# LSH attention with spatial gating: score tiles released by the minimum, two buffers of split rows, four of exponentials

## The chip, the cores and the metric

The kernel runs on one core of a Trainium2 chip. The metric is the device time of one execution in microseconds (us). A core has five engines with a program of their own each, run in order: TensorE (PE; its weight loads are listed as PEld), VectorE (DVE), ScalarE (ACT), GpSimd (POOL), and SyncE (SP), which here only issues transfers. TensorE writes to PSUM, a small memory of banks; everything else lies in SBUF. The kernel before took 742.45 us (median of 3 runs, 740.67 to 743.2).

## What is computed

Attention with 4 batches of 8 heads, 768 rows of 64 numbers. Each query and key gets a hash of 6 bits (signs of a projection), and a query sees only keys of its own hash. The outcome of all heads goes through a gated MLP with a product along the rows.

```python
q_bucket = np.sum((q @ proj > 0) * 2 ** np.arange(6), axis=-1)     # k_bucket alike
scores = np.where(q_bucket[..., :, None] == k_bucket[..., None, :], scale * q @ k.T, -1e9)
attn = np.exp(scores - np.max(scores, axis=-1, keepdims=True))
attn = attn / (np.sum(attn, axis=-1, keepdims=True) + 1e-09)
x = attn @ v                                                       # (4, 768, 512)
h = np.maximum(x @ w_in, 0.0)
u, v = h[..., :512], h[..., 512:]
v_n = (v - mean(v)) / np.sqrt(var(v) + 1e-06)
v_s = np.einsum('ts,bsd->btd', w_spatial, v_n) + b_spatial[None, :, None]
out = (u * v_s) @ w_out
```

## The kernel before

**Order.** The program is not written in the order in which it runs. Every step is registered with `op(engine, duration, function, predecessors, on=buffers, rank=...)`. `timetable` (line 117) then places all of them with the stated durations, each engine taking the ready operation of the lowest rank, and at the end the functions are called in the order of the planned starts. So each engine's order is fixed when the program is built; on the chip an engine runs its list in order and waits by semaphores for data and for buffers. A buffer is an object `buf(name, n)`: its `new()` waits for the users of the one `n` places before.

**Tiles.** Two heads make a pair, so there are 16 pairs (`p`), four to a batch. A pair has 6 steps (`i`), one for each 128 rows. `scores` (line 448) runs 16 products for a step, four passes over two halves of 384 columns for two heads: three with q and k split into fp16 parts (tile `hl`, from `split_qk`), one with hash rows (tile `hk`, from `hash_rows`), whose product puts other buckets far down. The outcome is one PSUM tile `sp` for each head, two banks each, and there are two of them, so that a step needs both tiles of the step before to be free.

**A step by queries** (`by_queries`, line 461): VectorE takes the minimum of the scores scaled by a negative factor (line 473, its elementwise output goes as bf16 into the `ex` tile and is not used); ScalarE takes the exponential of the scores, reading PSUM, into `ex` (line 476); ScalarE rounds it to fp16 in `pp` (line 480); VectorE or GpSimd writes the rest beside it (line 484); SP issues a transposing transfer `pt<-pp` (line 488); and some steps later `weighted` multiplies `pt` with the split `v` on TensorE (line 594). Heads 2, 4 and 6 (pairs 1 to 3) go by keys instead (`by_keys`), with a maximum found ahead (`row_max`) and an exponential straight from the scores (line 509).

**Buffers.** `ex` and `pp` have 3 each (`EB`, `PB`), `pt` 8 (`PTB`), `hl` 3, `hk` 3 tiles taken in turn. `load_qk` (line 302) brings q and k of a pair, one buffer.

**Ahead of a pair.** At step 1 of pair p `hash_rows(p + 2)` is registered, at step 2 `split_qk(p + 2)`, at step 3 `load_qk(p + 3)`. Hash rows go through TensorE and VectorE and are put into `hk` by 8 small transfers that GpSimd issues (line 356). After the last `weighted` of a pair comes `normalize`, in step 3 of the next pair.

**The MLP.** When a batch's four pairs are done, its products (`mlp_units`, all through line 689) are registered with a high rank number, so that the planner puts them where TensorE would be free. The last batch's products over its first three pairs are made beforehand (`partial_units`) and kept in tiles of `hl` and `qk`. The weights are brought and split by `weights()` from 30 us of the plan on.

Of the kernel before, what the change touches and what calls it, by code (L numbers as in the profile page):

```python
# [18 lines left out]
P = 128  # L19
D = 64  # L20
# [15 lines left out]
def lsh_attention_spatial_gating(  # L36
# [194 lines left out]
    ws = [const.tile([P, NT, S], F16, name=f"ws{i}") for i in range(2)]  # L231
# [4 lines left out]
    def weights():  # L236
# [5 lines left out]
        raws = buf("u", UB).new()  # L242
        vi, vo, vs = (x.rearrange("(c p) f -> p c f", p=P) for x in (w_in, w_out, w_sp))
# [7 lines left out]
        for i, (src, dst, m, f, key) in enumerate(jobs):  # L251
# [41 lines left out]

            t = op("A", 0.3 * z, high, t, on=hold, rank=R_W)
# [30 lines left out]
    def hash_rows(p, *after):  # L325
        qk, k = held["qk", p], buf("hk", NHK).new()
# [24 lines left out]
        for j in range(4):  # L351
            for e in range(2):
                q, eng = HQ_FIRST[e] if p == 0 else HQ_REST

                def move(j=j, e=e, eng=eng):
                    eng.dma_start(  # L356
                        out=hk[p % NHK][D * e:D * e + 2 * NB, 1 - j // 2, (j % 2) * HS:(j % 2 + 1) * HS],
                        in_=sg[1][32 * j + 16 * e:32 * j + 16 * e + 2 * NB, :])
                at["hk", p].append(op(q, 0.53 if q == "G" else 0.75, move, t, on=[g1, k], rank=3, land=2.8 if q == "G" else 1.8))

    def split_qk(p, *after):
        qk, h = held["qk", p], buf("hl", 3).new()
        held["hl", p] = h

        def high():
            st["hl", p] = wk.tile([P, 4, S], F16, tag="hl", bufs=3, name=f"hl{p}")
            nc.scalar.activation(st["hl", p][:, 1:3], st["qk", p], AF.Copy, scale=SQ)

        t = op("A", 1.42, high, at["qk", p], *after, on=[qk, h], rank=4)
        at["hl", p] = [t] + [  # L370
            op("V", 0.9, lambda to=to, part=part, frm=frm: nc.vector.scalar_tensor_tensor(
                out=st["hl", p][:, to], in0=st["qk", p][:, part], scalar=SQ, in1=st["hl", p][:, frm],
                op0=ALU.mult, op1=ALU.subtract), t, on=[qk, h], rank=4)
            for to, part, frm in ((0, 1, 2), (3, 0, 1))]
# [60 lines left out]
    def sums(ps, p, rows, passes, queries, halves=(0, 1), heads=(0, 1)):  # L435

        for a, (x, y, last) in enumerate(passes):
            for c in halves:
                cs = slice(c * HS, (c + 1) * HS)
                for e in heads:  # L440
                    byq_ = queries or 2 * p + e not in KEYS
                    r = slice(D * e, D * e + D - (last and byq_))
                    src = hk[p % NHK] if last else st["hl", p]
# [17 lines left out]
    def by_queries(p, i, e, g, t, sc):  # L461
# [6 lines left out]
        def low():  # L468
            if i == 0:
                st["nb", n] = wk.tile([P, NT], F32, tag="nb", bufs=6, name=f"nb{n}")  # L470
            ex = st["e32", n, i] = wk.tile([P, 2, HS], F32, tag="ex", bufs=EB, name=f"ex{n}_{i}")
            jk = ex.rearrange("p c k -> p (c k)").bitcast(BF16)[:, :S].rearrange("p (c k) -> p c k", c=2)
            nc.vector.tensor_scalar(jk, st["sc", p, i][e], -ISQ, None, op0=ALU.mult, op1=ALU.min, accum_out=st["nb", n][:, i:i + 1])  # L473

        def exp():
            nc.scalar.activation(st["e32", n, i], st["sc", p, i][e], AF.Exp, bias=st["nb", n][:, i:i + 1], scale=ISQ)  # L476
# [15 lines left out]
        t = op("A", 0.83, exp, t, on=[sc, hx], rank=(g, 0.1 + 0.1 * e))  # L492
# [52 lines left out]
    def max_row(p):  # L545
        for e in keys(p):
# [20 lines left out]
            def move(n=n, e=e):  # L567
                nc.sync.dma_start(out=hk[p % NHK][D * e + D - 1:D * e + D, 1, :], in_=st.pop(("mt", n)))

# [132 lines left out]
    def partial_units():  # L702
# [4 lines left out]
        hv_ = [buf("hl", 3).new() for _ in range(2)]  # L707
        hu = buf("qk", 1).new()
        held["vpart"], held["upart"] = hv_, hu
        on = [held["xt", b * NPAIR + c] for c in pairs]  # L710
        after = [at["xt", NP - 2]]

        for i in range(NT):
            def copy(c, i=i):
                if i % 3 == 0:
                    st["vb", i // 3] = wk.tile([P, 4, S], F16, tag="hl", bufs=3, name=f"vpart{i}").rearrange("p a s -> p (a s)").bitcast(F32)
# [5 lines left out]
        for d in range(NF):  # L722
            def copy(c, d=d):
                if d == 0:
                    st["ub"] = wk.tile([P, NF, HS], F32, tag="qk", name="upart")
                nc.scalar.copy(st["ub"][:, d], c[0])

            def then(t, c, pool, d=d, copy=copy):
                at["upart", d] = op("A", 0.4, lambda: copy(c), t, on=[hu], rank=1, gives=pool)
            group(f"upp{d}", HS, u_products(b, d, 0, pairs), then, on, after, bank_m, rank=8.9)  # L730

    def mlp_units(b):
# [102 lines left out]
        def u_unit(d, h):  # L835
# [9 lines left out]
            def then(t, c, pool):  # L845
                def plus():
                    make()
                    nc.vector.tensor_tensor(out=u[h][:, d], in0=c[0], in1=st["ub"][:, d], op=ALU.add)  # L848
# [6 lines left out]
                if part:  # L855
                    t = op("V", 0.45, plus, t, at["upart", d], on=[hu[h], held["upart"]], rank=1, gives=pool)
# [4 lines left out]
        def s_unit(d, h):  # L861
# [3 lines left out]
            if d == 0:  # L865
                hg[h] = (buf("hl", 3) if last and h else buf("g", 1)).new()
            hy = buf("sy", 2).new()

            def then(t, c, pool):
# [6 lines left out]
                def high():  # L876
                    if d == 0 and last and h == 1:
                        g1 = wk.tile([P, 4, S], F16, tag="hl", bufs=3, name="g_1").rearrange("p a s -> p (a s)")
# [41 lines left out]
    EB, PB, PTB, XTB, VB, UB = 3, 3, 8, 6, 6, 2  # L920
# [7 lines left out]
    R_W = 0.9  # L928
    W_FROM, W_EVERY = 30.0, 3.6
# [11 lines left out]
    weights()  # L941
# [6 lines left out]
    for g in range(STEPS + LAG):  # L948
# [15 lines left out]
        if p < NP:  # L964
# [79 lines left out]
```

## Time and profile before

| | before |
|---|---|
| median of 3 runs | 742.45 us |
| profiled execution, time | 743.31 us |
| profiled execution, span | 741.5 us |
| TensorE busy | 638.3 us |
| VectorE busy | 557.7 us |
| ScalarE busy | 459.4 us |
| GpSimd busy | 411.4 us |
| mean TensorE clock granted | 0.935 |

A row of a group of instructions reads: line, engine, operation, output<-inputs, sizes, count | busy us, mean ns of one | idle time of the engine just before them and who ended it. A row of waits reads: who waited <- for whom: us in total, times, longest. Names with a q (SPq) are an engine's queue. In a stage's row each engine has its busy us and its number of instructions, and then come the granted clock, the share of the DMA engines' time, and GB/s. A row of the timeline has start, duration, and in brackets the idle time before it.

### The profile page before, as it was taken

How to read it: one execution, taken by the hardware profiler on the slowest of the kernel's cores; microseconds unless marked ns; L12 is line 12 of the kernel's file. 1: busy time of each engine (PE TensorE's matmuls, PEld its weight loads, DVE VectorE, ACT ScalarE, POOL GpSimd, SP SyncE). 2: the span in 40 equal slices, each digit the busy share in tenths (PEclk: the TensorE clock that was granted, in tenths of full speed). 3: DMA queues.
4: the chain of work that ended last, by engine and by line, in shares of the span. 5: the costliest groups of instructions: out<-in, count | busy, mean ns of one | idle time of the engine just before them, and what ended most of it. 6: DMA issues, size and time to landing. Idle time of an engine off the chain costs nothing. (4 is left out here: it accounts for less than half of the span.)

```text
span 741.5 us, 16949 instructions
## 1 busy us (share of the span) xinstructions
PE 638.3 (86%) x6667; PEld 376.2 (51%) x6667; DVE 557.7 (75%) x1014; ACT 459.4 (62%) x707; POOL 411.4 (55%) x446
## 2 busy tenths in 40 slices
PE   3778799886988878698998799989889899989997
PEld 1445557563545455454554456545445555545553
DVE  6788987769999988877887989797968785382250
ACT  3767656777886865576676777676756775432212
POOL 5346665778657685856683858583745551233100
PEclk9889957887999998889999999999999999999999
DMA  5799784799998889799999789989698879001102
GB/s 179 148 167 203 165 177 100 159 226 177 188 202 145 150 179 188 160 181 204 172 181 184 155 174 175 185 177 204 128 173 172 135 128 163 3 1 44 44 1 85
DMA packets 318260, 110.85 MB, mean 149 GB/s; under 512 B 305124, under 2 KB 308196, under 8 KB 318180
## 3 DMA queue, kind: packets, MB, share of 16 engines
q1 hardware_dynamic: 314244, 108.62, 74.6%
q0 software_dynamic: 3840, 1.12, 0.8%
q8 instruction: 52, 0.85, 0.5%
q14 instruction: 28, 0.23, 0.1%
q10 hardware_dynamic: 96, 0.04, 0.0%
HBM read 27.94 MB, written 6.29 MB: 46 GB/s over the span
## 5 line engine op out<-in xcount | busy, mean ns | idle before, releaser
L476 ACT ACTIVATE ex<-sp,nb 128x768 f32<-128x768 f32 x174 | 155.0, 899 | 113.2 <-DVE ex L473 111.0
L484 POOL TENSOR_TENSOR pp<-ex,pp 128x768 f16<-128x768 f32 x66 | 116.8, 1770 | 109.7 <-ACT pp L480 107.3
L473 DVE TENSOR_SCALAR_CACHE_REDUCE ex<-sp 128x768 bf16<-128x768 f32 x174 | 160.0, 949 | 22.0 <-PE sp L445 20.2
L594 PE MATMUL pv<-vp,pt 128*128 128x65 f16 (+1 forms) x3132 | 125.3, 197 | 48.6 <-DMA pt<-pp 35.3
L484 DVE TENSOR_TENSOR pp<-ex,pp 128x768 f16<-128x768 f32 x108 | 126.2, 1174 | 53.3 <-ACT pp L480 53.0
L445 PE MATMUL sp<-hl 64*128 64x384 f16 x1152 | 137.7, 355 | 28.7 <-ACT ex L476 25.6
L594 PEld LDWEIGHTS <-pt 128*128 128x128 f16 x3132 | 111.7, 100 | 94.8 <-DMA pt<-pp 51.1
L480 ACT CAST pp<-ex 128x768 f16<-128x768 f32 x174 | 141.4, 828 | 22.6 <-DMA pt<-pp 22.2
L445 PEld LDWEIGHTS <-hl 64*128 64x128 f16 x1188 | 64.3, 100 | 93.5 <-issue 65.1
L689 PE MATMUL sps<-ws,vn 128*128 128x384 f16 x576 | 102.6, 330 | 0.7 <-DVE sy L874 0.5
L356 POOL DMA_DIRECT2D hk<-sg x120 | 64.1, 540 | 22.4 <-PE ups L689 7.4
L689 PEld LDWEIGHTS <-vn 128*128 128x128 f16 x576 | 54.8, 99 | 37.5 <-issue 4.8
L689 PE MATMUL ops<-wo,g 128*128 128x512 f16 x288 | 66.7, 381 | 1.9 <-DVE u L848 1.9
L886 POOL TENSOR_TENSOR sy<-sy,u 128x384 f32<-128x384 f32 x24 | 28.2, 1175 | 63.6 <-DVE sy L874 63.2
L445 PE MATMUL sp<-hk 63*128 63x384 f16 (+1 forms) x384 | 61.0, 355 | 2.8 <-DMA hk<-sg 2.8
L689 PE MATMUL ups<-xt,wi 128*128 128x384 f16 x348 | 61.5, 327 | 1.6 <-DVE sy L874 1.2
L689 PE MATMUL vps<-wi,xt 128*128 128x512 f16 x234 | 56.6, 380 | 1.9 <-DVE sg L341 1.1
L874 DVE SCALAR_TENSOR_TENSOR sy<-sps,bt 128x384 f32<-128x384 f32 x32 | 17.7, 552 | 43.9 <-PE sps L689 41.2
L689 PEld LDWEIGHTS <-wi 128*128 128x128 f16 x384 | 36.3, 98 | 26.0 <-issue 3.5
L882 ACT CAST g<-sy 128x384 f16<-128x384 f32 x32 | 16.4, 512 | 44.6 <-POOL sy L886 24.2
L689 PEld LDWEIGHTS <-g 128*128 128x128 f16 x288 | 26.9, 98 | 32.1 <-issue 3.1
L445 PEld LDWEIGHTS <-hk 63*128 63x128 f16 (+1 forms) x420 | 29.8, 104 | 24.0 <-issue 11.6
(103 smaller groups left out, 857.2 us busy)
## 6 DMA issues: line engine op xcount, KB each, us to landing
qk<-kq SPq DMA_DIRECT2D x16, 768.0 KB, 6.3
out<-o SPq DMA_DIRECT2D x24, 256.0 KB, 2.0
v<-v SPq DMA_DIRECT2D x13, 384.0 KB, 4.0
pt<-pp SPq DMA_TRANSPOSE x174, 4.6
raw<-w_in SPq DMA_DIRECT2D x8, 256.0 KB, 3.6
raws<-w_in SPq DMA_DIRECT2D x8, 256.0 KB
hk<-sg POOLq DMA_DIRECT2D x120, 9.0 KB, 3.3
vf<-v SPq DMA_DIRECT2D x3, 384.0 KB
```

What stands on the lines that cost most here:

```text
L356: eng.dma_start(out=hk[p % NHK][D * e:D * e + 2 * NB, 1 - j // 2, (j % 2) * HS:(j % 2 + 1) * HS], in_=sg[1][32 * j + 16 * e:32 * j + 16 * ...
L445: nc.tensor.matmul(ps[e][:, c - halves[0]], lhsT=src[r, l, rows], rhs=src[r, m, cs], start=(a == 0), stop=(a == len(passes) - 1))
L473: nc.vector.tensor_scalar(jk, st["sc", p, i][e], -ISQ, None, op0=ALU.mult, op1=ALU.min, accum_out=st["nb", n][:, i:i + 1])
L476: nc.scalar.activation(st["e32", n, i], st["sc", p, i][e], AF.Exp, bias=st["nb", n][:, i:i + 1], scale=ISQ)
L480: nc.scalar.copy(st["pp", n, i][:, 0], st["e32", n, i])
L484: eng.tensor_tensor(out=st["pp", n, i][:, 1], in0=st.pop(("e32", n, i)), in1=st["pp", n, i][:, 0], op=ALU.subtract)
L594: nc.tensor.matmul(o, lhsT=l, rhs=m, start=(i == 0 and k == 0), stop=(i == NT - 1 and k == len(todo_) - 1))
L689: nc.tensor.matmul(c[0], lhsT=l(), rhs=r(), start=(j == 0), stop=(j == len(products) - 1))
L874: nc.vector.scalar_tensor_tensor(out=y[0], in0=c[0], scalar=1.0 / (SN * SW), in1=bt[:, hs], op0=ALU.mult, op1=ALU.add)
L882: nc.scalar.copy(gt[h][0][:, d], y[0])
L886: t1 = op(*POST[last], lambda: either(t1).tensor_mul(y[0], y[0], u[h][:, d]), t, done["u", d, h], on=[hy, hu[h]], rank=2)
```

## The change

Four things are changed together. The minimum's instruction writes the scaled scores as fp32 into `ex`, and the exponential reads them there with a scale of -1; it no longer reads PSUM, so the next step's scores wait for the minimum alone. `ex` and `pp` get 4 buffers, `pt` 9. `hl` and `hk` get 2 buffers, with pair 1's rows in the tiles of the weights `ws`, which are written later; hashing and splitting of pair p + 1 is registered at step 0 of pair p (from pair 3 on), the load of pair p + 2 at step 1, and `weights()` after step 11. The last batch's partial sums are kept in other tiles (`hl`, `qk`, `v32`, `hk`).

```diff
-    NHK = 3
-    hk = [const.tile([P, 2, S], F16, name=f"hk{i}") for i in range(NHK)]
-    for i, t in enumerate(hk):
+    ws = [const.tile([P, NT, S], F16, name=f"ws{i}") for i in range(2)]
+    flat = [t.rearrange("p c s -> p (c s)") for t in ws]
+    hk = [const.tile([P, 2, S], F16, name=f"hk{i}") for i in range(2)]
+    hkt = lambda p: hk1 if p == 1 else hk[(p + 1) % 2 if p else 0]
+    hk1 = flat[1][:, :2 * S].rearrange("p (g s) -> p g s", g=2)
+    for i, t in enumerate(hk + [hk1]):
...
+        place = [buf("hl1", 1).new(), buf("hk1", 1).new()]
...
+            if key == "ws":
+                hold = hold + place
...
     def split_qk(p, *after):
-        qk, h = held["qk", p], buf("hl", 3).new()
+        qk, h = held["qk", p], (buf("hl", 2) if p != 1 else buf("hl1", 1)).new()
...
+            if p == 1:
+                st["hl", p] = flat[0][:, :4 * S].rearrange("p (g s) -> p g s", g=4)
+            else:
+                st["hl", p] = wk.tile([P, 4, S], F16, tag="hl", bufs=2, name=f"hl{p}")
...
-            jk = ex.rearrange("p c k -> p (c k)").bitcast(BF16)[:, :S].rearrange("p (c k) -> p c k", c=2)
-            nc.vector.tensor_scalar(jk, st["sc", p, i][e], -ISQ, None, op0=ALU.mult, op1=ALU.min, accum_out=st["nb", n][:, i:i + 1])
+            nc.vector.tensor_scalar(ex, st["sc", p, i][e], -ISQ, None, op0=ALU.mult, op1=ALU.min, accum_out=st["nb", n][:, i:i + 1])
 
         def exp():
-            nc.scalar.activation(st["e32", n, i], st["sc", p, i][e], AF.Exp, bias=st["nb", n][:, i:i + 1], scale=ISQ)
+            nc.scalar.activation(st["e32", n, i], st["e32", n, i], AF.Exp, bias=st["nb", n][:, i:i + 1], scale=-1.0)
...
-        t = op("A", 0.83, exp, t, on=[sc, hx], rank=(g, 0.1 + 0.1 * e))
+        t = op("A", 0.83, exp, t, on=[hx], rank=(g, 0.1 + 0.1 * e))
...
-        hv_ = [buf("hl", 3).new() for _ in range(2)]
-        hu = buf("qk", 1).new()
+        hv_ = [buf("hl", 2).new(), buf("qk", 1).new()]
+        hu = [buf("v32", 1).new(), buf("hk", 2).new()]
...
-    EB, PB, PTB, XTB, VB, UB = 3, 3, 8, 6, 6, 2
+    EB, PB, PTB, XTB, VB, UB = 4, 4, 9, 6, 6, 2
...
+    AHEAD = 1
...
-    weights()
...
-            if i == 1 and p + 2 < NP:
+            if i == AHEAD and p + 2 < NP and p < 2:
                 hash_rows(p + 2, now)
-            if i == 2 and p + 2 < NP:
                 split_qk(p + 2, now)
-            if i == 3 and p + 3 < NP:
+            if i == AHEAD + 1 and p + 3 < NP and p < 2:
                 load_qk(p + 3, now)
+            if i == 0 and 2 < p + 1 < NP and p > 2:
+                hash_rows(p + 1, now)
+                split_qk(p + 1, now)
+            if i == 1 and 4 < p + 2 < NP:
+                load_qk(p + 2, now)
+            if g == 2 * NT - 1:
+                weights()
```

More of the change, by code (lines that the diff above doesn't have):

```diff
@@ L356, in move @@
                     eng.dma_start(
[L357 removed]
+                        out=hkt(p)[D * e:D * e + 2 * NB, 1 - j // 2, (j % 2) * HS:(j % 2 + 1) * HS],
                         in_=sg[1][32 * j + 16 * e:32 * j + 16 * e + 2 * NB, :])
@@ L442, in sums @@
                     r = slice(D * e, D * e + D - (last and byq_))
-                    src = hk[p % NHK] if last else st["hl", p]
+                    src = hkt(p) if last else st["hl", p]
                     l, m = (x, y) if byq_ else (y, x)
@@ L715, in copy @@
                 if i % 3 == 0:
-                    st["vb", i // 3] = wk.tile([P, 4, S], F16, tag="hl", bufs=3, name=f"vpart{i}").rearrange("p a s -> p (a s)").bitcast(F32)
+                    t = (wk.tile([P, 4, S], F16, tag="hl", bufs=2, name=f"vpart{i}").rearrange("p a s -> p (a s)").bitcast(F32) if i == 0 else
+                         wk.tile([P, 2, S], F32, tag="qk", name=f"vpart{i}").rearrange("p a s -> p (a s)"))
+                    st["vb", i // 3] = t
                 nc.scalar.copy(st["vb", i // 3][:, (i % 3) * F2:(i % 3 + 1) * F2], c[0])
@@ L724, in copy @@
                 if d == 0:
-                    st["ub"] = wk.tile([P, NF, HS], F32, tag="qk", name="upart")
-                nc.scalar.copy(st["ub"][:, d], c[0])
+                    ub[0] = wk.tile([P, 2 * NT, D], F32, tag="v32", name="upart").rearrange("p a d -> p (a d)")
+                nc.scalar.copy(st["ub"](d), c[0])
             def then(t, c, pool, d=d, copy=copy):
-                at["upart", d] = op("A", 0.4, lambda: copy(c), t, on=[hu], rank=1, gives=pool)
+                at["upart", d] = op("A", 0.4, lambda: copy(c), t, on=[hu[d // 2]], rank=1, gives=pool)
             group(f"upp{d}", HS, u_products(b, d, 0, pairs), then, on, after, bank_m, rank=8.9)
@@ L847, in plus @@
                     make()
-                    nc.vector.tensor_tensor(out=u[h][:, d], in0=c[0], in1=st["ub"][:, d], op=ALU.add)
+                    nc.vector.tensor_tensor(out=u[h][:, d], in0=c[0], in1=st["ub"](d), op=ALU.add)
                 def relu():
@@ L855, in then @@
                 if part:
-                    t = op("V", 0.45, plus, t, at["upart", d], on=[hu[h], held["upart"]], rank=1, gives=pool)
+                    t = op("V", 0.45, plus, t, at["upart", d], on=[hu[h], held["upart"][d // 2]], rank=1, gives=pool)
                 done["u", d, h] = op("A", 0.4, relu, t, done.get(("u", 0, h)), on=[hu[h]], rank=1, gives=None if part else pool)
@@ L865, in s_unit @@
             if d == 0:
-                hg[h] = (buf("hl", 3) if last and h else buf("g", 1)).new()
+                hg[h] = (buf("hl", 2) if last and h else buf("g", 1)).new()
             hy = buf("sy", 2).new()
@@ L877, in high @@
                     if d == 0 and last and h == 1:
-                        g1 = wk.tile([P, 4, S], F16, tag="hl", bufs=3, name="g_1").rearrange("p a s -> p (a s)")
+                        g1 = wk.tile([P, 4, S], F16, tag="hl", bufs=2, name="g_1").rearrange("p a s -> p (a s)")
                         gt[h] = [g1[:, k * NF * HS:(k + 1) * NF * HS].rearrange("p (d q) -> p d q", d=NF) for k in range(2)]
```

8 lines of the change are left out of this document (4 added, 4 removed).

## The prediction

> **What bounds the kernel now.** I read the page's head, the stages, TensorE's waits, one step in the timeline, and then who is late on the engines that feed it. The page's span and engine sums, and the stages by window (length, busy time and count of each engine, granted TensorE clock, DMA share, GB/s):
>
> ```profile
> span 741.5 us, 16949 instructions
> PE 638.3 (86%) x6667; PEld 376.2 (51%) x6667; DVE 557.7 (75%) x1014; ACT 459.4 (62%) x707; POOL 411.4 (55%) x446
> ...
> 0.00:12.00 12.00, 3.94 (x20) 1.06 (x22) 8.13 (x12) 3.78 (x4) 6.46 (x17) 1.00 0.48 170
> 12.00:52.00 40.00, 26.65 (x315) 15.84 (x313) 30.69 (x61) 25.00 (x34) 15.65 (x19) 0.85 0.84 167
> 52.00:160.00 108.00, 93.30 (x908) 65.06 (x902) 86.77 (x181) 70.69 (x125) 73.29 (x90) 0.82 0.81 164
> 160.00:473.00 313.00, 268.65 (x3145) 156.21 (x3144) 266.20 (x463) 221.40 (x331) 213.59 (x220) 0.94 0.93 178
> 473.00:625.00 152.00, 136.68 (x1639) 78.88 (x1639) 121.14 (x215) 103.88 (x151) 82.40 (x81) 0.99 0.88 162
> 625.00:742.00 117.00, 109.11 (x655) 59.12 (x651) 44.78 (x86) 34.63 (x67) 19.97 (x20) 0.99 0.11 36
> ```
>
> The rows cut the run into start-up, pair 0, pairs 1 to 3 (by keys), 4 to 11, 12 to 15, and a tail. The tail is TensorE alone: 109 of 117 us busy, DMA at 0.11. What it runs are products of the MLP that the attention found no room for. So any gap of TensorE closed during the attention shortens the tail or the attention by as much: the end is TensorE's work, 638.3, plus its gaps, 741.5 - 638.3 = 103.2 us. No other engine is full: from 12 to 625 VectorE is busy 504.8 of 613 us, ScalarE 421.0. The question is which gaps close. TensorE's waits (total, times, longest):
>
> ```profile
> PE pv L594 <- DMA pt<-pp: 35.3, 32, 4.5
> PE sp L445 <- ACT ex L476: 25.6, 30, 4.2
> PE pv L594 <- DVE x L623: 12.9, 8, 2.9
> PE hp L334 <- DMA qk<-kq: 5.8, 1, 5.8
> ...
> PE sp L445 <- ACT ex L509: 2.8, 2, 2.1
> ```
>
> The second row is the wait that the first part of the change is aimed at: the next scores wait for the exponential (L476) that still reads the old ones. One such step in the timeline (start, duration):
>
> ```profile
> 184.46 0.94 DVE L473 TENSOR_SCALAR_CACHE_REDUCE ex<-sp 128x768 bf16<-128x768 f32 x1
> ...
> 185.33 0.94 DVE L473 TENSOR_SCALAR_CACHE_REDUCE ex<-sp 128x768 bf16<-128x768 f32 x1
> 185.44 1.78 ACT L476 ACTIVATE ex<-sp,nb 128x768 f32<-128x768 f32 x2 [2.91 <-DVE ex L473]
> ...
> 186.39 0.32 PE L445 MATMUL sp<-hl 64*128 64x384 f16 x1 [2.33 <-ACT ex L476]
> ...
> 187.27 2.07 PE L445 MATMUL sp<-hl 64*128 64x384 f16 x11 [0.56 <-ACT ex L476]
> ```
>
> The first minimum ends at 185.40 and TensorE gets that tile at 186.39; the second ends at 186.27, its tile is taken at 187.27. Released by the minimum, with the same 0.05 us of hand-over (185.40 to 185.44), a tile is free about 0.94 us sooner.
>
> **The change part by part.** The groups it touches (count, busy, mean ns, idle before and its releaser):
>
> ```profile
> L476 ACT ACTIVATE ex<-sp,nb 128x768 f32<-128x768 f32 x174 | 155.0, 899 | 113.2 <-DVE ex L473 111.0
> L473 DVE TENSOR_SCALAR_CACHE_REDUCE ex<-sp 128x768 bf16<-128x768 f32 x174 | 160.0, 949 | 22.0 <-PE sp L445 20.2
> L484 DVE TENSOR_TENSOR pp<-ex,pp 128x768 f16<-128x768 f32 x108 | 126.2, 1174 | 53.3 <-ACT pp L480 53.0
> L480 ACT CAST pp<-ex 128x768 f16<-128x768 f32 x174 | 141.4, 828 | 22.6 <-DMA pt<-pp 22.2
> ...
> L371 DVE SCALAR_TENSOR_TENSOR hl<-qk,hl 128x768 f16<-128x768 f32 x32 | 34.7, 1107 | 0.8 <-ACT hl L367 0.8
> L367 ACT ACTIVATE hl<-qk 128x1536 f16<-128x1536 f32 x16 | 23.7, 1479 | 4.2 <-DMA qk<-kq 3.7 <-issue 0.5
> L623 DVE TENSOR_TENSOR x<-pv,rv 128x384 f32<-128x384 f32 x32 | 16.8, 547 | 0.1
> L509 ACT ACTIVATE ex<-sp 128x768 f32<-128x768 f32 x18 | 14.5, 803 | 17.8 <-PE sp L445 17.7
> ```
>
> (1) Score tiles are released by the minimum. Thirty waits of 25.6 us lose up to 0.94 us each. In the timeline eight of them are longer (the longest keeps 4.2 - 0.94 = 3.3, the quoted 2.33 keeps 1.4); together they keep 7.3 us. Gain 25.6 - 7.3 = **18.3 us**; bounds 0 (all of it turns up as a wait elsewhere) and 25.6. The 2.8 behind L509 stays, as heads by keys keep their exponential on the scores. What is late next is VectorE's minimum itself, which in program order stands behind its other work.
>
> (2) The exponential reads SBUF. Nearest rows: a 128x768 pass of ScalarE took 803 ns from PSUM (L509, without a bias tile) and 828 from SBUF (L480), so 25 ns more, 174 times: 4.4 us of ScalarE, which idles 113 us in front of these very instructions. I take 0 on the path, bounds 0 and 4.4, the latter if that idle time were gone. [...]
>
> (3) The minimum writes 768 f32 in place of 768 bf16. No row shows this instruction with f32. L623 reads PSUM and writes f32: 547 ns for 384 elements; L473 takes 949 for 768. The 384 more cost 402 ns, about 1.05 ns an element whichever type is written. I take no change; bounds 0 and the 225 ns by which L484, f32 operands of the same size on VectorE, exceeds it (1174), which is 39 us over 174.
>
> (4) A fourth `pp` and `ex` and a ninth `pt`. The cast (L480) waits 22.2 us, 22 times, about 1.0 us each, for a transpose to have read the `pp` of three tiles before. With four it waits for the transpose one place earlier: 128x1536 f16 are 393 KB, 2.2 us at the 178 GB/s of the middle stage (an estimate), more than the mean wait, so nearly all of it goes. The way to TensorE:
>
> ```profile
> SPq L488 <- DVE pp L484: 118.8, 58, 8.4
> ...
> SPq L308 <- DVE hl L371: 8.0, 3, 4.9
> ```
>
> SP's queue, which issues the transposes, waits 118.8 us for the rest (L484); this waits 53.0 for the cast (its row above); the cast 22.2 for buffers. Of VectorE's 53.0, 22.2 at most is of this origin, 42%; of TensorE's 35.3 behind transposes that is 14.8. I take half of the 22.2, **11 us**; bounds 0 and 22.2.
>
> (5) Split rows and hash rows in two buffers. Nothing is added: as many hash products, splits and DMA issues. From pair 4 on they move from steps 1, 2 and 3 of the pair two before to steps 0 and 1 of the pair just before. The chain to be ready in time:
>
> ```profile
> qk<-kq SPq DMA_DIRECT2D x16, 768.0 KB, 6.3
> ...
> hk<-sg POOLq DMA_DIRECT2D x120, 9.0 KB, 3.3
> ...
> L356 POOL DMA_DIRECT2D hk<-sg x120 | 64.1, 540 | 22.4 <-PE ups L689 7.4
> ```
>
> Eight issues on GpSimd are 4.3 us, the landing 3.3, the split 1.5 + 2 x 1.1 = 3.7; one after the other 11.3 us. The lead was eleven steps and is six; a step of pairs 4 to 15 takes (625 - 160) / 72 = 6.5 us, so 39 us remain. The buffer that is written was last read by the step just before, already past on TensorE, so the eight issues hold nothing on GpSimd's queue that they do not hold now. The `qk` load goes by SP's queue: it waits there for the split (L371), with transposes behind it: 8.0 us in 3 of 16 loads today. The distance between split and load stays one step, so I take 0; bounds 0 and 16 us, if each of the 11 loads from pair 5 on waited the longest 4.9 (54 us) and TensorE felt 35.3 / 118.8 of it. On the other side, today hash, split, load, the `v` split and the normalisation crowd steps 1 to 3; spread out they could gain some us, which I don't count.
>
> (6) Pair 1's rows lie in `ws`, and the weights come after them in the list. The last scores of pair 1 in the timeline, and the first writes of `ws` (min/median/max, first and last start):
>
> ```profile
> 80.00 0.48 PE L445 MATMUL sp<-hk 64*128 64x384 f16 x2
> ...
> L292 ACT ACTIVATE ws<-raw x6: 507/520/525, 122.4 to 162.4; 128x384 f16<-128x384 f32 x6
> ```
>
> They end at 80.5 us and the writes begin at 122.4: no wait. The partial sums of the last batch go to other tiles whose readers are done by then; 0.
>
> **Sum.** The profiled execution took 743.3 us (741.5 of span and 1.8 around it); 743.3 - 18.3 - 11 = **714 us**. The median of the runs shown, 742.45, is 0.9 below that execution; the range covers it.
>
> **The rivals.**
>
> *The clock comes back as well.* TensorE was granted 0.85, 0.82 and 0.94 in three stages and 0.99 after. At 1.00 their matmuls lose 0.15 x 26.65 + 0.18 x 93.3 + 0.06 x 268.65 = 37 us. If shorter gaps restore half, the time is 714 - 18 = 696. For it: 0.99 where TensorE is 90% busy (136.68 of 152), 0.94 where it is 86%. Against it: it was granted 0.62 in a stretch without any gap:
>
> ```profile
> 100.00:125.00 25.00, 25.00 (x181) 16.87 (x181) 18.67 (x42) 12.65 (x21) 12.64 (x13) 0.62 0.64 140
> ```
>
> [...] Chance 0.13.
>
> *The transposes take the wait over.* DMA is at 0.93 from 160 to 473. If scores come sooner but transposes land no sooner, term 4 gives nothing and a fifth of term 1 returns as waits of L594: 743.3 - 18.3 x 0.8 = 729. For it: the largest wait is already theirs. Against it: SP's queue waits for data 118.8 us. Chance 0.16.
>
> *The change doesn't shorten anything.* The planner's pace (`T_QUERIES` and the rest) is unchanged, so as many MLP products stand between two steps in TensorE's order; only 25.6 of 103.2 us of gaps name the exponential. If both terms just move to other rows: 741 to 745. Chance 0.09.
>
> *Slower: the f32 write shares a path with GpSimd.* The place is L473, on the loop scores, minimum, scores. L484 on VectorE averages 1174 ns, GpSimd working beside it; were L473 to go to the same, 174 x 0.225 = 39 us come onto the loop: 714 + 39 = 753. It decides from 29.3 / 174 = 0.17 us on, a mean of 1.12 us. Against it: L623's f32 writes (547) show no such excess. Chance 0.10.
>
> **How the numbers follow.** Forecast 0.52, clock 0.13, transposes 0.16, nothing 0.09, slower 0.10. About 0.3% is what a measurement of this kernel can tell from no change. Faster 0.52 + 0.13 + 0.16 = 0.81, same 0.09, slower 0.10. The forecast's own bounds are 743.3 - 25.6 - 22.2 = 695 and 714 + 16 + 4 = 734. The range goes from 692, into the clock's case, to 742, into the nothing's; left out are the slower case and the edges of two, under 0.2.
>
> **What would show it.** `PE sp <- ACT ex L476` is gone, and a wait for `DVE ex` of at most 8 us stands there. L480's wait for transposes falls under 6 us, L594's from 35 to about 24. L476 takes 920 to 945 ns, L473 still 949. TensorE's busy time stays at 638 within 6. L473 above 1.12 us, a `qk` load that waits for L371 for more than 2 us in most pairs, or L594's wait grown beyond 45 us would each prove me wrong.

## The result and the profile after

The changed kernel took 748.18 us (median of 20 runs, 741.99 to 757.74), the kernel before 741.35 on the same chip (median of 20); the ratio is 1.013, with a 95% interval of 1.0095 to 1.0165. It is slower by 1.3%, where 714 us were forecast. The medians here and below are of all runs, while the ratios leave out the slow executions of a kernel, so a ratio need not be the quotient of the two medians beside it. The profiled execution took 750.24 us. Head of the page after, then its stages, cut as those of before were:

```profile
span 748.4 us, 16873 instructions
...
PE 631.0 (84%) x6667; PEld 370.7 (50%) x6667; DVE 558.5 (75%) x1009; ACT 463.5 (62%) x707; POOL 419.0 (56%) x451
```

```profile
12.00:52.00 40.00, 28.38 (x311) 16.41 (x308) 34.81 (x65) 25.38 (x34) 25.54 (x30) 0.81 0.85 176
52.00:160.00 108.00, 91.52 (x989) 64.31 (x988) 94.06 (x189) 76.77 (x127) 63.05 (x77) 0.90 0.81 166
160.00:473.00 313.00, 258.40 (x3115) 150.75 (x3112) 260.93 (x455) 220.24 (x331) 208.25 (x211) 0.95 0.93 177
473.00:625.00 152.00, 132.91 (x1566) 75.09 (x1563) 116.64 (x207) 100.86 (x145) 95.89 (x96) 0.97 0.85 157
625.00:749.00 124.00, 115.94 (x688) 63.03 (x684) 43.98 (x85) 36.44 (x70) 19.86 (x20) 1.00 0.12 36
```

TensorE works 7.3 us less than before (631.0 for 638.3; the granted clock's mean is 0.945 for 0.935), and its gaps grew from 103.2 to 748.4 - 631.0 = 117.4 us. Length less TensorE's time, stage by stage: from 160 to 473 us 44.4 before and 54.6 after, from 473 to 625 us 15.3 and 19.1. The windows are the same in time, not in work. Cut at the work instead, from the first scores of pair 4 to the last scores of all, the rows are these, before and after:

```profile
160.30:619.40 459.10, 399.89 (x4721) 232.27 (x4722) 383.60 (x670) 321.61 (x476) 294.94 (x299) 0.95 0.91 172
```

```profile
146.90:618.50 471.60, 393.82 (x4711) 227.78 (x4712) 384.51 (x673) 328.85 (x486) 312.39 (x318) 0.95 0.92 173
```

TensorE's gaps there are 59.2 us before and 77.8 after. So the loss lies in pairs 4 to 15, which go by queries and which the change was made for. TensorE's largest waits after (total, times, longest), then those of SP's queue for a transpose's data and for the split:

```profile
PE pv L601 <- DMA pt<-pp: 49.5, 41, 2.5
PE sp L453 <- DVE ex L480: 16.1, 19, 1.8
PE pv L601 <- DVE x L630: 15.6, 9, 5.2
...
SPq L495 <- DVE pp L491: 79.2, 46, 5.2
...
SPq L313 <- DVE hl L379: 11.2, 4, 4.1
```

The wait for the exponential is gone, as forecast, and what stands in its place is the minimum, 16.1 us for 25.6. But the products with transposes, which waited 35.3 us, wait 49.5, although SP's queue now waits 79.2 us for VectorE's rest in place of 118.8. The groups that were touched:

```profile
L483 ACT ACTIVATE ex<-ex,nb 128x768 f32<-128x768 f32 x174 | 158.0, 934 | 120.8 <-DVE ex L480 120.5
L480 DVE TENSOR_SCALAR_CACHE_REDUCE ex<-sp 128x768 f32<-128x768 f32 x174 | 160.0, 949 | 24.9 <-PE sp L453 24.8
L491 DVE TENSOR_TENSOR pp<-ex,pp 128x768 f16<-128x768 f32 x103 | 126.4, 1231 | 57.7 <-ACT pp L487 56.7
L487 ACT CAST pp<-ex 128x768 f16<-128x768 f32 x174 | 138.4, 822 | 0.6
```

The cast's 22.2 us of waits for buffers have become 0.6 us of idle time, but the next link, VectorE's wait for the cast, is no shorter (53.0 before, 56.7 now), and ScalarE waits 120.5 us for the minimum where it waited 111.0. The waits moved along the chain.

**Where the attention stood.** The first scores of pair 4 in the trace before (matmuls: min/median/max in ns, first and last start), and after:

```profile
L445 PE MATMUL sp<-hl x12: 497/524/524, 160.3 to 161.8; 64*128 64x384 f16 x12
```

```profile
L453 PE MATMUL sp<-hl x12: 319/322/333, 146.9 to 148.2; 64*128 64x384 f16 x12
```

There the change's execution was 13.4 us ahead, and in a phase of a higher clock (322 ns for 524 in the median; granted were 1.00 from 146.9 to 148.3 us, and 0.50 from 160 to 162 before). Not all of this lead need be the change's. Three kernels below (e9, e10, e11) run the program of before up to pair 4, and their executions reach it at 156.6, 152.1 and 152.6 us. They were granted clocks of 0.88, 0.94 and 0.89 over the first 152 us, where the execution of before had 0.84 over its first 160. So 3.7 to 8.2 us of the 13.4 can be the execution alone. The last scores of all in the timeline before, and after:

```profile
619.37 1.15 PE L445 MATMUL sp<-hl 64*128 64x384 f16 x12
```

```profile
618.48 1.15 PE L453 MATMUL sp<-hl 64*128 64x384 f16 x12
```

The lead is down to 0.9 us. What is left to do then is products of the MLP. The windows of their line alone (length, TensorE busy and count, weight loads, clock, DMA, GB/s), before and after:

```profile
0.00:619.00 619.00, 192.37 (x941) 86.13 (x942) 0.92 0.88 171
619.00:742.00 123.00, 109.86 (x597) 57.71 (x595) 0.99 0.17 43
```

```profile
0.00:618.00 618.00, 185.03 (x892) 82.52 (x893) 0.93 0.88 171
618.00:749.00 131.00, 117.68 (x645) 62.56 (x643) 1.00 0.15 40
```

The attention took as long as before with some 48 products fewer among its steps, and these lie behind it. From the last scores to the end are 122.1 us for 594 products before and 129.9 for 642 after, 0.206 and 0.202 us for each. How many products stand ahead of the last scores is settled by TensorE's order, which the planner fixes when the program is built.

### The profile page after: what moved, and what is told of

It reads as the page before. It is cut to its first block, busy times and chain, and to the rows that moved or that the text cites. A ratio compares the mean times of both kernels' runs of the same rounds, so it can differ in the third digit from the quotient of the medians.

```text
span 748.4 us, 16873 instructions
## 1 busy us (share of the span) xinstructions
PE 631.0 (84%) x6667; PEld 370.7 (50%) x6667; DVE 558.5 (75%) x1009; ACT 463.5 (62%) x707; POOL 419.0 (56%) x451
## 4 chain that ended last, share of the span: by engine, by line
PE 27%; DVE 21%; DMA 13%; issue 10%; ACT 6%; POOL 6%; DVEq 0%; SPq 0%; ACTq 0%; POOLq 0%
DMA pt<-pp 12%; PE sps L696 6%; DVE ex L480 6%; PE ops L696 6%; PE sp L453 4%; DVE pp L491 4%; PE pv L601 4%; ACT pp L487 3%; ACT ex L483 2%; PE ups L696 2%; POOL pp L491 2%; DVE hl L379 2%; PE vpp L696 2%; DVE vr L828 1%; PE vps L696 1%
## 5 line engine op out<-in xcount | busy, mean ns | idle before, releaser
L483 ACT ACTIVATE ex<-ex,nb 128x768 f32<-128x768 f32 x174 | 158.0, 934 | 120.8 <-DVE ex L480 120.5
L601 PE MATMUL pv<-vp,pt 128*128 128x65 f16 (+1 forms) x3132 | 128.3, 198 | 63.7 <-DMA pt<-pp 49.5
L480 DVE TENSOR_SCALAR_CACHE_REDUCE ex<-sp 128x768 f32<-128x768 f32 x174 | 160.0, 949 | 24.9 <-PE sp L453 24.8
L491 POOL TENSOR_TENSOR pp<-ex,pp 128x768 f16<-128x768 f32 x71 | 125.2, 1765 | 88.6 <-ACT pp L487 82.2
L491 DVE TENSOR_TENSOR pp<-ex,pp 128x768 f16<-128x768 f32 x103 | 126.4, 1231 | 57.7 <-ACT pp L487 56.7
L487 ACT CAST pp<-ex 128x768 f16<-128x768 f32 x174 | 138.4, 822 | 0.6
L453 PE MATMUL sp<-hl 64*128 64x384 f16 x1080 | 118.7, 345 | 16.9 <-DVE ex L480 15.6
L453 PEld LDWEIGHTS <-hl 64*128 64x128 f16 x1104 | 54.0, 98 | 72.3 <-issue 46.1
L361 POOL DMA_DIRECT2D hk<-sg x112 | 59.5, 537 | 43.1 <-PE ups L696 16.0
L633 POOL TENSOR_TENSOR x<-x,xf 128x384 f32<-128x384 f32 x31 | 39.3, 1267 | 26.7 <-DVE x L630 25.9
L453 PE MATMUL sp<-hk 63*128 63x384 f16 (+1 forms) x360 | 51.5, 345 | 2.7 <-DMA hk<-sg 2.7
L893 ACT CAST g<-sy 128x384 f16<-128x384 f32 x32 | 16.3, 510 | 42.7 <-POOL sy L897 22.2
```

Source lines behind the costliest of these rows:

```text
L361: eng.dma_start(out=hkt(p)[D * e:D * e + 2 * NB, 1 - j // 2, (j % 2) * HS:(j % 2 + 1) * HS], in_=sg[1][32 * j + 16 * e:32 * j + 16 * e + 2 ...
L453: nc.tensor.matmul(ps[e][:, c - halves[0]], lhsT=src[r, l, rows], rhs=src[r, m, cs], start=(a == 0), stop=(a == len(passes) - 1))
L480: nc.vector.tensor_scalar(ex, st["sc", p, i][e], -ISQ, None, op0=ALU.mult, op1=ALU.min, accum_out=st["nb", n][:, i:i + 1])
L483: nc.scalar.activation(st["e32", n, i], st["e32", n, i], AF.Exp, bias=st["nb", n][:, i:i + 1], scale=-1.0)
L487: nc.scalar.copy(st["pp", n, i][:, 0], st["e32", n, i])
L491: eng.tensor_tensor(out=st["pp", n, i][:, 1], in0=st.pop(("e32", n, i)), in1=st["pp", n, i][:, 0], op=ALU.subtract)
```

## The experiments

The theories carry letters in the expectations, and each says there what it holds; the two that were left at the end are D (the moved steps crowd the engines at the wrong place) and H (the four edits are worth little, and the time is that of the order that the planner happens to find). Line numbers shift by a few between kernels.

### The minimum alone, and the change without two of its parts

e1 gives the kernel before the new minimum and exponential and keeps its order.

```diff
-            jk = ex.rearrange("p c k -> p (c k)").bitcast(BF16)[:, :S].rearrange("p (c k) -> p c k", c=2)
-            nc.vector.tensor_scalar(jk, st["sc", p, i][e], -ISQ, None, op0=ALU.mult, op1=ALU.min, accum_out=st["nb", n][:, i:i + 1])
+            nc.vector.tensor_scalar(ex, st["sc", p, i][e], -ISQ, None, op0=ALU.mult, op1=ALU.min, accum_out=st["nb", n][:, i:i + 1])
...
-            nc.scalar.activation(st["e32", n, i], st["sc", p, i][e], AF.Exp, bias=st["nb", n][:, i:i + 1], scale=ISQ)
+            nc.scalar.activation(st["e32", n, i], st["e32", n, i], AF.Exp, bias=st["nb", n][:, i:i + 1], scale=-1.0)
```

> The kernel before with the new minimum and the exponential from SBUF alone; buffers, and the order of every engine, are those of before (the planner is still told that the exponential holds the score tiles; 942 MLP products stand ahead of the last scores, as before). Theory A (the loss comes from the new order that the planner makes, with 894 MLP products ahead of the last scores where 942 stood; releasing the score tiles sooner is worth its waits): the waits for the exponential, 25.6 us, go and about half of them reach the end, 728 to 736 us, ratio 0.98 to 0.993. Theory B (score tiles don't set the pace of pairs 4 to 15; what is freed there comes back as waits for transposes): the exponential's row goes, the transposes' row grows by as much, 739 to 744 us, ratio 0.997 to 1.003. Theory C (the minimum's f32 write or the exponential from SBUF costs by itself): above 745 us.

In e2 the planner, too, knows that the exponential no longer holds the scores, and makes its order by that.

```diff
-        t = op("A", 0.83, exp, t, on=[sc, hx], rank=(g, 0.1 + 0.1 * e))
+        t = op("A", 0.83, exp, t, on=[hx], rank=(g, 0.1 + 0.1 * e))
```

> As the run before it, but the planner is told of the sooner release, so the order changes; 942 MLP products ahead of the last scores. Theory A: as the run with the same order, within 5 us, since the number of products ahead of the last scores stays. Theory B: 739 to 746 us. Theory C: above 745 us.

e3 takes these edits back from the change, the planner's line too. e4 takes back the counts of buffers, as follows. Both orders are made anew.

```diff
-    EB, PB, PTB, XTB, VB, UB = 4, 4, 9, 6, 6, 2
+    EB, PB, PTB, XTB, VB, UB = 3, 3, 8, 6, 6, 2
```

> The whole change except the new minimum: exponential from PSUM, bf16 output of the minimum; buffers 4, 4, 9, two of hl and hk; 894 MLP products ahead of the last scores. Theory A: the order costs its 48 products, so 748 to 760 us, no better than the change itself, ratio 1.01 to 1.025. Theory B: 747 to 751, the same as the change. Theory C: back to 741 or below.

> The change with 3 buffers of ex and pp and 8 of pt; 903 MLP products ahead of the last scores. Theory A: products as in the change, so 745 to 752 us, and the wait of the cast for transposes is back at about 20 us. Theory B: 748 to 756 us, since the buffers are what the change gained. If the fourth buffers themselves do the harm (weighted sums placed sooner in TensorE's order): 738 to 744 us, with TensorE's wait for transposes back from 49 to about 35 us.

e1 took 743.1 us against 741.15, ratio 1.0033 (1.0005 to 1.0061); e2 742.73, 1.0044 (1.001 to 1.0078). TensorE's waits in e1, and its exponential:

```profile
PE pv L593 <- DMA pt<-pp: 42.9, 35, 5.3
PE sp L445 <- DVE ex L472: 14.7, 12, 5.0
...
PE mx L445 <- DVE mx L540: 6.2, 8, 1.8
```

```profile
L475 ACT ACTIVATE ex<-ex,nb 128x768 f32<-128x768 f32 x174 | 160.2, 933 | 110.9 <-DVE ex L472 110.5
```

Against the kernel before, with the same order, the scores' wait lost 25.6 - 14.7 = 10.9 us; the transposes' gained 7.6 and that for the maximum 2.8. By these rows next to nothing is left. Scores that come sooner don't make the rest of the step sooner, and TensorE then waits at its next appointment. The three rows don't tell all: by the head of its page TensorE's gaps in e1 are 110.2 us in all for 103.2, and its matmuls take 630.0 us for 638.3 at a higher mean clock (0.941 for 0.935). So what settles it is the time, which did not fall: the first part of the change is worth nothing by itself, at most a loss of 0.6%. Theory B's ranges held in both runs; theory A's 728 to 736 us for e1 did not.

e3 took 764.35 us (1.0286, 1.0225 to 1.0347) and e4 761.56 (1.0297, 1.0255 to 1.0339), slower than the change itself and above every range that was given for them. In e4 the cast's wait for transposes came back at 12.6 us, where about 20 were expected, and TensorE's stayed at 50.7, so nothing speaks for the fourth buffers as the harm. Taken alone, the two times would say that the minimum and the buffers are worth about 1.6% each inside the change. It can't be read so, as the order was made anew both times (e16 below).

### The moved steps, and the loads

e5 is the kernel before with the change's steps for hashing, splitting and loading (the block of the diff at the top that begins with `AHEAD`, without the move of `weights()`); it keeps its own three buffers. e6 is the change with the steps put back from pair 3 on, as far as two buffers allow:

```diff
-            if i == 0 and 2 < p + 1 < NP and p > 2:
+            if i == 1 and 2 < p + 1 < NP and p > 2:
                 hash_rows(p + 1, now)
+            if i == 2 and 2 < p + 1 < NP and p > 2:
                 split_qk(p + 1, now)
-            if i == 1 and 4 < p + 2 < NP:
+            if i == 3 and 4 < p + 2 < NP:
                 load_qk(p + 2, now)
```

> The kernel before, its three buffers and old minimum, but hashing, splitting and loading registered at the change's steps (for pair p+1 at steps 0 and 1 of pair p); the planner puts 903 products ahead of the last scores, not 942. Theory D (the new steps for hash, split and load are what costs: they crowd step 0, delay what follows, and the plan fills TensorE less): 758 to 772 us, ratio 1.02 to 1.04, as the change without its gains. Rival E (the two buffers, the weights' place or the partial sums' tiles cost, not the steps): 738 to 746 us.

> The change, with hashing of pair p+1 at step 1, splitting at step 2 and loading at step 3 of pair p (from pair 3 on) where the change has 0, 0 and 1; two buffers as in the change; 948 products ahead of the last scores. Theory D: the loss of the change goes and its gains stay: 725 to 737 us, ratio 0.98 to 0.995. Rival E: 745 to 752, as the change.

e7 and e8 are the kernel before and e1 with 64 KB in place of 768 KB for each load from pair 5 on; these pairs then work with pair 4's rows, so the output is another.

```diff
     def load():
+            if p > 4:
+                st["qk", p] = st["qk", 4]
+                nc.sync.dma_start(out=st["qk", p][:, 0, 0:P], in_=kq[b, r][:, 0, 0:P])
+                return
```

> The kernel before, in which pairs 5 to 15 use pair 4's q and k again and load 64 KB each where 768 KB came, so the output is another; order and all other work as before. Theory B (transposes, so the DMA engines, set the pace of pairs 4 to 15): 8.4 MB less at 178 GB/s is 43 us of transfers less; TensorE's wait for transposes falls below 25 us and the time to 715 to 730 us. If DMA is not the bound there: 736 to 742 us.

> The new minimum in the order of before, with the light loads of the run before it. Theory B: with the DMA engines relieved the sooner release now shows: 8 to 18 us below the old minimum with light loads, where with full loads it was 2 us above. If the release is worth nothing for another reason: within 4 us of the old minimum with light loads.

e5 took 752.99 us against 740.79: 1.0143 (1.0086 to 1.02). The moved steps alone, with none of the buffers or the minimum, cost as much as the whole change, in the new order that the planner makes of them (903 products ahead of the last scores). The time lies between the two ranges that were given. e6 took 738.13: 0.9961 (0.9921 to 1.0001), the change with the steps put back, just above theory D's 725 to 737 us. TensorE's waits in e6, and its products of the MLP up to the last scores:

```profile
PE pv L601 <- DMA pt<-pp: 40.4, 40, 2.8
PE sp L453 <- DVE ex L480: 20.0, 24, 3.0
```

```profile
0.00:610.00 610.00, 194.85 (x947) 87.08 (x948) 0.94 0.88 173
```

Its last scores come 9 us sooner than those of before (610.3 for 619.4), with 948 products ahead of them for 942.

The light loads gained nothing: e7 740.53 us, 1.0046 (1.0 to 1.0092); e8 742.64, 1.0028 (0.9987 to 1.0069), beside 1.0033 for e1. The transposes' wait in e8 is that of e1 (42.9):

```profile
PE pv L597 <- DMA pt<-pp: 42.8, 35, 5.8
```

In e7 it is 37.7 us, for 35.3 before. So the theory that the loads press on the transposes fell: the wait has its name from a transfer, but 11 x 704 KB less traffic (7.7 MB, not the 8.4 of the expectation) does not shorten it.

### What an engine's time is worth

Three kernels put work into the kernel before that the planner doesn't know of, so the order stays: 48 times 384 elements in pairs 4 to 15, on VectorE in steps 1 to 4 (e9), on VectorE in steps 5 and 0 (e10), on ScalarE in steps 1 to 4 (e11). The lines that e9 adds behind the minimum, and then those of e11 behind the exponential; in e10 it is `range(2 ...)` with `not 0 < i < 5`.

```diff
+            for _ in range(1 if e and p > 3 and 0 < i < 5 else 0):
+                nc.vector.reduce_max(xacc, wide1, axis=AX.X)
...
+            if e and p > 3 and 0 < i < 5:
+                nc.scalar.activation(xtra, wide1, AF.Copy, scale=2.0)
```

> The kernel before, order unchanged, with one more VectorE instruction behind the second minimum of steps 1 to 4 of pairs 4 to 15: a maximum over 384 elements whose result is not used, about 0.55 us, 48 times, 26 us of VectorE. Theory F (VectorE sets the pace in these steps, where it is busy 0.85 to 0.93, so a score tile given back sooner finds VectorE late): 759 to 769 us, ratio 1.024 to 1.037. Theory G (no engine alone; a little of everything): 748 to 757.

> As the run before it, but two such instructions in each of the steps 5 and 0 of pairs 4 to 15, the same 26 us in all, where VectorE is busy 0.73. Theory F: most of it fits into idle time, 742 to 752 us. Theory G: 748 to 757, as in steps 1 to 4.

> The kernel before, order unchanged, with one more ScalarE copy of 384 elements, about 0.5 us, behind the second exponential of steps 1 to 4 of pairs 4 to 15, 24 us of ScalarE. Theory F: ScalarE is 0.70 busy but its cast stands between the minimum and VectorE's rest, so a third of it at most, 741 to 750 us. Theory G: 748 to 757.

What was added, in the groups of e9 and of e11:

```profile
L477 DVE TENSOR_REDUCE xacc<-ones 128x1 f32<-128x384 f32 x48 | 26.2, 545 | 0.0
```

```profile
L480 ACT ACTIVATE xtra<-ones 128x384 f32<-128x384 f32 x48 | 24.6, 514 | 0.0
```

e9 came out at 1.0142 (1.0068 to 1.0216), which is 10.5 of 738.28 us for 26.2 us of work; e10 at 1.0068 (1.0027 to 1.0109), 5.0 for 26.4; e11 at 1.0094 (1.0046 to 1.0142), 6.9 for 24.6. None arrives whole and none is free: about 0.4, 0.2 and 0.3 of it reach the end, though from 160 to 625 us VectorE idles 78 of 465 us and ScalarE 140 (by the stages before). e9 fell into theory G's range, e10 and e11 into F's. My reading is that no engine alone is the bound, and that several of them, each in a fixed order, are late in turn. This speaks for a part of theory D too: VectorE's time in steps 1 to 4 seems dearer than in steps 5 and 0, though the two intervals overlap.

### The order alone

Theory D says that the old steps are good and the new ones bad. Theory H says that any small number of the planner would do the same. e12 is the change, and e13 is e6, with a planned pace of 5.75 in place of 5.8 us a step; e14 is the change, and e15 the kernel before, with `LOOK`, the planner's patience for a better operation, at 0.05 in place of 0.2. The functions that are called are the same; their order is another, and with it which of the rests (L491) go to GpSimd and which to VectorE, since the planner gives each to the engine that is free.

```diff
-    T_FIRST, T_KEYS, T_QUERIES, T_LAST = 5.0, 4.8, 5.8, 5.8
+    T_FIRST, T_KEYS, T_QUERIES, T_LAST = 5.0, 4.8, 5.75, 5.75
...
-    LOOK = 0.2
+    LOOK = 0.05
```

> The change as it is, its steps for hash, split and load too, with the planner's pace of pairs 4 to 15 at 5.75 us a step in place of 5.80: buffers and instructions are the same, another order comes out, with 951 MLP products ahead of the last scores where the change has 894. Theory H (the loss is the order that the planner happened to find: every product left behind the attention is paid in the tail, about 0.18 us each by the change and the run with the old steps): 735 to 742 us, ratio 0.992 to 1.001. Theory D (the crowded step 0 costs by itself): 745 to 752 us, as the change.

> The change with the old steps 1, 2 and 3 for hash, split and load, and the pace of 5.75 us: 885 products ahead of the last scores, where 948 stood at 5.80. Theory H: slow in spite of the old steps, 746 to 755 us, ratio 1.006 to 1.02. Theory D: 735 to 741 us, as with the old steps at 5.80.

> The change, its steps kept, with the planner looking 0.05 us ahead in place of 0.20 when it picks the next operation: 1005 products ahead of the last scores. Theory H: 110 more than the change at 0.18 us, 726 to 735 us, ratio 0.978 to 0.992, below both kernels. Theory D: 744 to 752 us.

> The kernel before with the same look ahead of 0.05 us: 897 products ahead of the last scores where it had 942. Theory H: 746 to 754 us, ratio 1.006 to 1.018, though nothing of the change is in it. Theory D: 738 to 744 us.

e12 took 740.25 us against 741.81: 0.9968 (0.9925 to 1.001). The change with its moved steps is as fast as the kernel before once the planner's pace is 1% shorter. Its products up to the last scores:

```profile
0.00:620.00 620.00, 193.66 (x951) 86.52 (x951) 0.94 0.89 171
```

e13 took 747.9: 1.012 (1.0065 to 1.0175). With the steps put back, which gave 0.996 in e6, it is as slow as the change. The order of e15 alone costs the kernel before 1.0223 (1.0168 to 1.0278), 756.72 us, more than theory H's 746 to 754. So D alone is not the cause, and H gave the right sign in three of four: the time goes with the order, whichever steps it was made from. The products in e13 up to the last scores, and behind them:

```profile
0.00:613.00 613.00, 186.88 (x885) 81.12 (x885) 0.92 0.90 172
613.00:747.00 134.00, 120.41 (x651) 63.66 (x651) 0.98 0.14 39
```

e14 missed: 748.72 us, 1.0108 (1.0053 to 1.0162), no faster than the change, though more products than in any other run lie among its steps:

```profile
0.00:639.00 639.00, 206.97 (x1005) 90.66 (x1005) 0.92 0.86 166
```

Its last scores come at 638.8, 19 us later than before, for 63 products more. The count alone decides nothing. Why this order is slow among the steps was not followed up.

### The wait put back, and an order made to fit

e16 is the change with the old minimum in the change's own order (the two lines of e1, taken back, without the planner's). e17 is e6 with `LOOK` at 0.1. e18 is e6 with one number of the planner made later: how long after its place in SP's queue it takes a transfer, a transposed tile above all, to have landed. The same number holds for the other transfers of that queue.

```diff
-    LOOK = 0.2
+    LOOK = 0.1
...
-                come = queue[0] + 0.25
+                come = queue[0] + 1.5
```

> The change in its own order (894 products, the planner told that the minimum frees the score tiles) with the old minimum and the exponential from PSUM: only the wait is put back. In the order of before the sooner release was worth nothing (743.1 us with it, 741.2 without). If it is worth nothing here too: 746 to 750 us, as the change. If an order that was made for the sooner release needs it: 756 to 770 us, near the change replanned for the old minimum (764).

> A search for a faster version: the change with the old steps 1, 2, 3 and a look ahead of 0.10 us; 972 products ahead of the last scores, 24 more than e6. At 0.205 us a product and if the last scores come as in e6 (610 us): 730 to 738 us, ratio 0.985 to 0.997. If the last scores come late as in e14: 742 to 750 us.

> The same search: the change with the old steps and the planner counting a transpose as landed 1.5 us after its transfer in place of 0.25, so that weighted sums stand later in TensorE's order; 960 products. TensorE's wait for transposes falls below 35 us; 728 to 738 us, ratio 0.982 to 0.997. If the wait doesn't fall, 738 to 745 us.

e16 took 752.51 us against 742.55: 1.0154 (1.0097 to 1.0211), beside 1.013 (1.0095 to 1.0165) for the change. In one order the new minimum gains 0.2%, within both intervals, and not the 1.6% that e3 suggested; the time itself lies between the two ranges that were given. TensorE's waits in e16:

```profile
PE pv L602 <- DMA pt<-pp: 35.5, 32, 2.7
PE sp L453 <- ACT ex L484: 34.1, 34, 2.6
PE pv L602 <- DVE x L631: 11.3, 5, 3.8
```

From here to the change, the scores' wait loses 18.0 us (34.1 to 16.1), the transposes' gains 14.0 (35.5 to 49.5) and the normalised rows' 4.3 (11.3 to 15.6): 0.3 us more in all. It is e1's exchange over again, in another order.

e17 took 735.63: 0.9923 (0.9886 to 0.9961), with 972 products ahead of last scores at 609.9. Its transposes' wait is larger than the change's:

```profile
PE pv L601 <- DMA pt<-pp: 53.6, 53, 4.0
```

So the sum of a wait is no measure of an order either. e18 took 724.15 us (719.37 to 730.86): 0.976 (0.97 to 0.982), the fastest of all, 2.4% below the kernel before and, by the two ratios (0.976 / 1.013), 3.7% below the change. Its waits, its last scores and its products:

```profile
PE pv L601 <- DMA pt<-pp: 24.5, 26, 2.8
PE sp L453 <- DVE ex L480: 19.8, 28, 3.3
```

```profile
601.50 1.15 PE L453 MATMUL sp<-hl 64*128 64x384 f16 x12
```

```profile
0.00:601.00 601.00, 196.38 (x959) 87.86 (x960) 0.94 0.91 176
```

Against e6, which differs in that one number, the wait for transposes fell from 40.4 to 24.5 us and the last scores come 8.8 us sooner, with 12 products more ahead of them. It is also faster than its forecast of 728 to 738 us. That the planner now asks for tiles when they are there is the plain reading. How much of the 2% between e6 and e18 is that, and how much the luck of one more order, one run can't tell; the late landing was not tried on the kernel before, so the share of the change in e18 is open too.

### All orders in one table

Start of the last scores and products ahead of and behind it, each from its own profiled execution (times in us); the end is worked out as that start + 0.205 for each product behind.

| kernel | ratio to before | last scores | products ahead / behind | end worked out | span |
|---|---|---|---|---|---|
| before | 1 | 619.4 | 942 / 594 | 741.2 | 741.5 |
| after | 1.013 | 618.5 | 894 / 642 | 750.1 | 748.4 |
| e1 | 1.003 | 618.0 | 942 / 594 | 739.8 | 740.2 |
| e2 | 1.004 | 619.8 | 942 / 594 | 741.6 | 743.5 |
| e3 | 1.029 | 624.1 | 894 / 642 | 755.7 | 755.6 |
| e4 | 1.030 | 628.3 | 903 / 633 | 758.1 | 758.3 |
| e5 | 1.014 | 622.3 | 903 / 633 | 752.1 | 753.5 |
| e6 | 0.996 | 610.3 | 948 / 588 | 730.8 | 732.8 |
| e12 | 0.997 | 620.0 | 951 / 585 | 739.9 | 742.5 |
| e13 | 1.012 | 612.8 | 885 / 651 | 746.3 | 746.4 |
| e14 | 1.011 | 638.8 | 1005 / 531 | 747.7 | 747.8 |
| e15 | 1.022 | 620.9 | 897 / 639 | 751.9 | 751.9 |
| e16 | 1.015 | 615.5 | 894 / 642 | 747.1 | 745.3 |
| e17 | 0.992 | 609.9 | 972 / 564 | 725.5 | 727.7 |
| e18 | 0.976 | 601.5 | 960 / 576 | 719.6 | 723.0 |

The end worked out lies within 4 us of the span in every row. (e12's profiled execution took 744.24 us, above its median.) A product among the steps saves 0.205 us behind them. What it costs there is what an order decides; that it is nothing in a gap and up to its full time where it holds up a step is my reading, and no run prices a single product.

The same can be read from the heads of the pages, as length less TensorE's time. TensorE's gaps in all are 95.9 us in e18, 103.2 before, 104.7 in e6, 104.9 in e17, 110.2 in e12, 115.5 in e15, 117.4 after, 117.8 in e5, 120.6 in e3 and 125.2 in e4. So the slow orders are roughly those in which TensorE waits longest. The match is not exact, since TensorE's time moves with the clock from one execution to the next (622.8 us in e17 at 0.950, 643.2 in e2 at 0.926).

## Why the prediction was wrong

**The step that failed** stands in the first part: "any gap of TensorE closed during the attention shortens the tail or the attention by as much", with every term then added to the end, and with it term 5's nought for moved steps. It took TensorE's order as given and its gaps as independent, so that a wait that goes leaves the others as they are. Both were wrong: the end is still TensorE's work plus its gaps (631.0 + 117.4 us after), but the minimum's release took nothing from the end in a fixed order (e1, 1.0033), and the new order has 48 products fewer among its steps, some 10 us of work that is left for the tail.

**Term 1, 18.3 us.** The mechanism went as described (the wait for the exponential is gone), the size of the wait that goes was half (25.6 to 16.1; at most 8 us were to remain), and the gain was nothing: in one and the same order e1 measures a ratio of 1.0033, and e16 against the change 0.2% the other way. What is late next was named as the minimum alone. It was TensorE's next appointments, the transposes above all (7.6 of 10.9 us in e1, 14.0 of 18.0 in e16). The rival in which transposes take the wait over had the right row and gave it a fifth of the term; it was about three quarters, and other rows took the rest. One of the prediction's own signs of being wrong came true here: that wait is 49.5 us, beyond the 45 it named. TensorE's busy time, 631.0 us, also left the 638 within 6.

**Term 2, nought on the path.** The exponential takes 934 ns for 899, inside the 920 to 945 forecast: 35 ns, 174 times, is 6.1 us of ScalarE. The rows of before gave 25 ns (924 ns, and 4.4 us as the bound), so the bound was too low; no run shows the forecast's upper end of 945. The term's cover is thinner than was said: e11 has about 0.3 of such work on ScalarE reach the end, though in steps 1 to 4 only. That share of 6.1 us is 1.7 us, which may be a part of the 0.3% in e1 (2.4 us); it was not tried alone.

**Term 3, nought.** Right: the minimum takes 949 ns with f32 as with bf16, and the rival that was slower for this reason fell. The sign was that rival's, the mechanism not.

**Term 4, 11 us.** The cast's wait went as forecast, 22.2 to under 1 us. The next step, that 42% of VectorE's wait for the cast is of this origin, failed: that wait is 56.7 us after 53.0. By the profile none of the 11 us arrived. No run has the buffers alone in a fixed order, so their worth is not measured; e6, which has them and the minimum, is 0.4% faster than before, in an order of its own.

**Term 5, nought.** This is where the time went. The queue was judged rightly: the `qk` load waits 11.2 us in 4 loads for the split, where it was 8.0 in 3. But moving registered steps makes the planner place everything anew, and with these steps it found orders with fewer products among the steps, 39 fewer in e5 (1.0143, with no other edit) and 48 in the change. In a new order any of the four edits could have done it, and a 1% shorter pace undoes it (e12). What makes one order slower than another among the steps stays open (e14).

**Term 6, nought.** The early part of the profiled execution is faster, 13.4 us at pair 4, which the prediction didn't foresee. A part of that, 3.7 to 8.2 us, shows between executions of the old program too; which edit brought the rest, if one did, was not tried.

**The rivals.** "Doesn't shorten anything" (741 to 745) is what the minimum alone does, 743.1, and its reason, that the planner's pace and so the products between two steps decide, was the right one; but it was taken as a reason for no change, when the planner is free to move either way.

## What to carry to other kernels

Where a planner or a list sets each engine's order, a change of one registration, buffer count or duration is two changes, the edit and a new order: hold the order and change the edit (e1, e16), then hold the edit and change the order (e12, e15), before giving either the credit. A removed wait is worth its time only if what the engine waits for next is already there (10.9 us of waits gone in e1, and a ratio of 1.0033), so follow the chain to the next appointment on that engine before adding the term. And where orders alone spread by some per cent, first bring the planner's numbers closer to the trace, as e18 did in one run, and then compare edits over several orders each.

## What the runs showed of the hardware that was not expected

**Waits that carry a transfer's name.** Median time from issue to landing of the transposes (174 of them), after and in e18:

```profile
pt<-pp SPq DMA_TRANSPOSE x174, 4.1
```

```profile
pt<-pp SPq DMA_TRANSPOSE x174, 4.9
```

They land later after their issue in e18, and TensorE waits half as long for them (24.5 us for 49.5). Here the wait says when TensorE asked, not how fast the transfer is.

**The clock.** TensorE's gaps grew by 14 us (103.2 to 117.4) and its granted clock rose (0.935 to 0.945). Its three longest gaps were 5.8, 4.5 and 4.2 us before and 5.9, 5.2 and 2.7 after, so the added gaps are short ones. The clock also differs between executions of one order: e10, in the order of before, had 0.959 and gaps of 115.1 us. In both pairs the larger sum of gaps stands beside the higher clock.

**Orders.** With the same functions called, two orders (with the choice between VectorE and GpSimd in them) differ by 1.6% (the change and e12) and by 2.2% (before and e15), which is more than any single edit did in a fixed order.
